# Row sums stored with a step, a guard on one engine, and a new order list in a two-layer attention kernel

## The chip, the cores and the metric

The kernel runs on one core of a Trainium2 chip, as one program in one launch. Its time is the device time in microseconds (us) of that core. What is compared is the median over runs of each kernel. One execution was also taken with the hardware profiler; its rows are what is read below.

The core has TensorE (matrix products into PSUM), VectorE, ScalarE and GpSimd (elementwise work; GpSimd doesn't reach PSUM) and SyncE, whose queue SP issues nearly all the DMAs here. In the rows they are PE (its weight loads PEld), DVE, ACT, POOL and SP.

## What is computed

The first layer is an attention with sinks and a window, 4 batches of 8 heads, 768 positions of 64 values; the second is a mixture of 4 attention experts over its result, of which each row takes the best two.

```python
keep = is_sink | in_window                 # 4 sinks, window 128
scores = np.where(keep, scale * q @ k.T, -1e9)
a = np.exp(scores - scores.max(-1))
a = a / (a.sum(-1) + 1e-9)
x = a @ v                                  # first layer, all heads side by side: 768 x 512
...
logits = x @ w_gate                        # 4 experts, the best 2 kept, softmax over them
for e in range(4):                         # causal attention of each expert
    q, k, v = x @ wq[e], x @ wk[e], x @ wv[e]
    a = exp(masked(scale * q @ k.T) - max)
    a /= a.sum(-1) + 1e-9
    out += weight[e] * (a @ v @ wo[e])
```

All is in float32. The `1e-9` under each row sum is the *guard* of this document.

## The kernel before, in words

**Work units.** The first layer goes by pairs of heads (16 of them: 4 batches of 4), each in blocks of 128 rows. Rows 0 and 1 of a pair form one unit (`first_rows`, L1051), rows 2 and 3, and 4 and 5, one each (`both_rows`, L1112). The second layer goes by pairs of experts (8 of them): `first_rows` for rows 0 and 1, `wide_rows` (L940) for rows 2 to 5. In each unit TensorE makes scores in PSUM (L713, L721, L730); VectorE masks them and takes the row minimum of the negated scores (`low`, L987, L1069, L1131); ScalarE takes the exponential and the row's sum (`exp`, L999, L1074, L1135); then comes the factor; GpSimd or ScalarE multiplies by it (L1007, L1009, L1086, L1089, L1155); and the result is transposed, either by TensorE (L791) with evacuations, or by VectorE and a trip through DRAM (out L834 and L926, back L838 to L923), for the product with v (L757, L762). Batch 0 of the first layer comes first, with its q and k transposed by TensorE (`turn_by_pe`, L683); after that a batch's second layer lies beside the next batch's first. The second layer's projections are three-pass products (L1244 for q and k, L1271 for v, L1320 for the output).

**The row statistics.** Each unit holds one tile `st` of 128 partitions by 20 values (six exist), seen as 5 rows of 4: row 0 the minimum, row 1 the sum, row 2 the factor, row 3 a partial minimum. A row has 2 or 4 values in use, side by side. Row 4 is filled with 1e-9 at the start (L465) and nothing reads it. The factor is made by `factor` (L770) in two steps, and in the second layer by a third: the guard adds 1e-9 to the 2 or 4 sums, on VectorE or GpSimd as the list says; VectorE takes the reciprocal; GpSimd multiplies by the row's expert weight:

```python
on = nc.gpsimd if guarded.eng == POOL else nc.vector
on.tensor_scalar(st.t[:, 2, :w], st.t[:, 1, :w], 1e-9, None, op0=OP.add)
...
nc.vector.reciprocal(st.t[:, 2, :w], st.t[:, 2, :w])
```

**The order.** Each piece of work is a step of a planner (`plan.step`), with a cost in ns for each engine that may do it; there are 2514. The text `ORDER` names them all in the order in which they are issued. A letter behind a number chooses the engine (`a` ScalarE, `v` VectorE, `p` GpSimd) or, with `q`, another tile shape on TensorE; without one the step goes to the first engine of its costs. Every engine takes its own steps in that order and waits at each for what it needs. So the list alone sets what is queued behind what. The costs, the waits for a DMA to land (`lag`, `BACK_LATE`, `LOAD_LATE`) and the clock that `emit` (L259) keeps from them serve to make a list; with a list given they still set which buffer a step gets and where spare products (L373, L375) go while TensorE would be idle.

**TensorE's tile shapes.** A step has a mode: `quad` works on 64x64 tiles, four side by side; `rows` and `ROWS` on two halves of the rows; `cols` on two halves of the columns; `FULL` on the whole array. The product with the sinks (L762) may be `FULL` or `rows`.

## Time and profile before

| | |
|---|---|
| runs shown | 346.21, 346.69, 346.72 us |
| median | 346.69 us |
| profiled execution | 345.65 us |
| its span, first to last instruction | 343.9 us |
| granted TensorE clock, mean over the span | 1.000 |
| busy in the span: TensorE, VectorE, ScalarE, GpSimd | 98%, 83%, 76%, 63% |
| guards on VectorE, on GpSimd | 39, 49 |

Busy shares are means over stages with different limits. TensorE counts as busy while a product is under way, and the ends of products are modelled, so a second look by stretch is needed. A row of the grouped view gives line, engine, operation, destination<-source by tile name, shapes and count, then the busy time in us and the mean duration in ns of one, and behind the second bar the engine's idle time just before them and who ended it. In the view of one line the three numbers are the shortest, the middle and the longest duration in ns. A row of the timeline gives the start and the length in us, and in brackets the idle time before it.

### The profile page before, as it was taken

To read this page: it belongs to the slowest core of one execution; us is meant where nothing else is said; L and a number is where in the kernel's file an instruction comes from. 1 tells how busy PE (TensorE), PEld (TensorE's weight loads), DVE (VectorE), ACT (ScalarE), POOL (GpSimd) and SP (SyncE) were. 2 spreads that over 40 slices of the span, in tenths; PEclk is the share of its full clock that TensorE was granted. 3 is DMA by queue.
4 is the path that set the end of the run, shared out by engine and by line. 5 is a ranking of instruction groups with operands and counts; after the bars stand their busy time and mean duration, and the time that the engine had idled before them with its cause. 6 is when DMAs were issued, how large, how long until landed. Compare 5 with 4: busy or idle time off the path is not lost.

```text
span 343.9 us, 12484 instructions
## 1 busy us (share of the span) xinstructions
PE 336.1 (98%) x4292; PEld 292.9 (85%) x4292; DVE 285.6 (83%) x1198; ACT 263.1 (76%) x871; POOL 216.9 (63%) x481
## 2 busy tenths in 40 slices
PE   8989999999999999999999999999999999999996
PEld 7777888987997889988889889987898899987885
DVE  4999999889998997899896997898888964489721
ACT  3999999879968978479868874599958868259822
POOL 6789998987956747758683744287687700285500
PEclk9999999999999999999999999999999999999999
DMA  6999589797968779878966778759775283057667
GB/s 179 248 202 163 99 166 171 177 205 182 300 181 203 248 178 156 234 152 173 279 194 131 218 225 181 231 110 254 231 211 181 80 266 126 2 191 202 208 201 274
DMA packets 159319, 65.45 MB, mean 190 GB/s; under 512 B 115856, under 2 KB 148880, under 8 KB 159256
## 3 DMA queue, kind: packets, MB, share of 16 engines
q1 hardware_dynamic: 158984, 64.53, 74.1%
q8 instruction: 34, 0.56, 0.7%
q14 instruction: 29, 0.24, 0.2%
q10 hardware_dynamic: 272, 0.13, 0.1%
HBM read 39.69 MB, written 24.90 MB: 188 GB/s over the span
## 4 chain that ended last, share of the span: by engine, by line
PE 82%; POOL 6%; DMA 4%; DVE 2%; ACT 2%; issue 1%; SPq 1%; ACTq 0%; POOLq 0%; DVEq 0%
PE b L757 20%; PE b L1244 20%; PE b L1320 10%; PE b L1271 8%; PE b L721 7%; PE b L791 6%; PE b L730 5%; PE b L713 2%; PE b L762 2%; DMA n<-in_v_dram 1%; DMA n<-in_q_dram 1%; POOL n L1089 1%; DMA p<-d 1%; POOL p L1155 1%; SPq L1198 1%
## 5 line engine op out<-in xcount | busy, mean ns | idle before, releaser
L1135 ACT ACTIVATE p<-p,st 128x132 f32<-128x132 f32 x128 | 51.0, 404 | 0.4 <-DVE st L1131 0.2
L1074 ACT ACTIVATE n<-n,st 128x128 f32<-128x128 f32 (+1 forms) x96 | 42.9, 449 | 4.1 <-DVE st L1069 3.9
L721 PE MATMUL b<-ks,qs 64*128 64x384 f32 (+3 forms) x384 | 39.6, 336 | 0.0
L1089 POOL TENSOR_TENSOR n<-n,st 128x256 f32<-128x256 f32 (+2 forms) x48 | 33.8, 714 | 4.9 <-DVE st L779 3.8
L1271 PE MATMUL b<-wvh,x 128*128 128x260 f32 x192 | 36.4, 284 | 0.0
L999 ACT ACTIVATE n<-n,st 128x768 f32<-128x768 f32 (+1 forms) x32 | 28.1, 878 | 10.5 <-DVE st L987 10.2
L776 POOL TENSOR_SCALAR st<-st 128x4 f32<-128x4 f32 (+1 forms) x49 | 11.0, 224 | 37.3 <-ACT n L999 19.2
L757 PE MATMUL b<-n,v 128*64 128x128 f32 x544 | 34.1, 274 | 0.2 <-issue 0.2
L1320 PE MATMUL b<-woh,y 128*128 128x512 f32 (+1 forms) x100 | 34.2, 396 | 0.0
L1155 POOL TENSOR_TENSOR p<-p,st 128x512 f32<-128x512 f32 x32 | 33.3, 1046 | 0.2
L721 PEld LDWEIGHTS b<-ks,qs 64*128 64x128 f32 x384 | 31.1, 186 | 2.5 <-issue 0.7
L1244 PE MATMUL b<-x,wqh 128*128 128x256 f32 (+1 forms) x128 | 32.9, 342 | 0.3 <-DVE st L987 0.3
L1244 PE MATMUL b<-x,wkh 128*128 128x512 f32 (+1 forms) x128 | 33.2, 343 | 0.0
L1131 DVE CUSTOM_DVE_ANT_0 p<-b,pair_mask 128x132 f32<-128x132 f32 x128 | 32.2, 284 | 0.2
L757 PEld LDWEIGHTS b<-n,v 128*64 128x64 f32 x544 | 30.2, 137 | 2.1 <-issue 1.4
L609 ACT ACTIVATE n<-b 128x384 f32<-128x384 f32 (+2 forms) x65 | 26.7, 439 | 7.0 <-PE b L683 4.6
L1271 PEld LDWEIGHTS b<-wvh,x 128*128 128x128 f32 x192 | 30.2, 188 | 0.7 <-DVE st L1069 0.4
L932 POOL TENSOR_SCALAR_AFFINE_SELECT p<-p 128x256 f32<-128x256 f32 x48 | 21.0, 461 | 14.0 <-DMA p<-d 13.6
L831 DVE STREAM_TRANSPOSE n<-n 128x768 f32<-128x768 f32 (+1 forms) x32 | 28.2, 897 | 1.1 <-ACT n L1007 0.5
L609 ACT ACTIVATE p<-b 128x256 f32<-128x256 f32 (+2 forms) x53 | 22.4, 447 | 8.0 <-PE b L1320 7.3
L730 PE MATMUL b<-n,n 64*64 64x196 f32 (+1 forms) x512 | 27.4, 337 | 0.0
L702 DVE STREAM_TRANSPOSE n<-n 128x384 f32<-128x384 f32 x48 | 26.7, 563 | 0.8 <-DMA n<-in_k_dram 0.8
(147 smaller groups left out, 1028.4 us busy)
## 6 DMA issues: line engine op xcount, KB each, us to landing
d<-n SPq DMA_DIRECT2D x24, 288.0 KB
n<-in_v_dram SPq DMA_DIRECT2D x16, 384.0 KB
p<-d SPq DMA_DIRECT2D x96, 64.0 KB
d<-n SPq DMA_DIRECT2D x16, 384.0 KB
n<-d SPq DMA_DIRECT2D x64, 96.0 KB
out_dram<-p SPq DMA_DIRECT2D x23, 256.0 KB
d<-n SPq DMA_DIRECT2D x16, 320.0 KB
n<-d SPq DMA_DIRECT2D x64, 80.0 KB
```

Source lines behind the costliest of these rows:

```text
L609: nc.scalar.activation(dst(), src(), AF.Copy)
L721: nc.tensor.matmul(o, self.qs.t[hs, a, qs], x, start=n == 0, stop=n == 2)
L730: nc.tensor.matmul(o[c:c + 64, 256 * r:256 * r + n], self.q_of()[hs, q:q + 64], self.ks.t[hs, 0, k:k + n], start=True, stop=True)
L757: nc.tensor.matmul(o[e * 64:e * 64 + 64], lhs, rhs, start=e not in self.begun, stop=last and self.done == len(self.steps))
L1074: nc.scalar.activation(x, x, AF.Exp, bias=st.t[:, 0, n:n + 1], scale=-1.0, accum_out=st.t[:, 1, n:n + 1])
L1089: nc.gpsimd.tensor_mul(x, x, f[:, :, None].to_broadcast([128, n, 128 * i + 128]))
L1131: nc.vector.tensor_tensor_reduce(out=p.t[:, n, :], in0=s2[e].t[:, 324 * r:324 * r + SW], in1=pair_mask, scale=-scale, scalar=BIG, op0=OP.a ...
L1135: nc.scalar.activation(p.t[:, n, :], p.t[:, n, :], AF.Exp, bias=st.t[:, 0, n:n + 1], scale=-1.0, accum_out=st.t[:, 1, n:n + 1])
L1155: nc.gpsimd.tensor_mul(p.t[:, :, :128], p.t[:, :, :128], f()[:, :, None].to_broadcast([128, 4, 128]))
L1244: nc.tensor.matmul(t.t, w[a][:, c, es], X[b, c].t[:, x, cs], start=c == 0 and m == 0, stop=c == NCH - 1 and m == 2)
L1271: nc.tensor.matmul(t.t[:, :VW], X[b, c].t[:, a, qs], W["wv"][w][:, c, :], start=c == 0 and n == 0, stop=c == NCH - 1 and n == 2)
L1320: nc.tensor.matmul(t.t[:, a0:z0], Y[b, c].t[:, a, qs], W["wo"][w][:, c, a0:z0], start=c == 0 and n == 0, stop=c == EP - 1 and n == 2)
```

## The change

- The tile `st` is seen through a new function `stats`: value n of row r lies at 5n + r, so the 2 or 4 values of a row are 20 bytes apart. All three makers of `st` use it. The six fills of row 4 go.
- The guard is always on VectorE. The planner's costs of guard and reciprocal, of `clean` and of the band's second mask get new numbers.
- `first_rows` of the first layer may, by `q` in the list, make its scores in 64x64 tiles (`quarters`): two column halves, one after the other, in place of one.
- The planner takes loads of q, k and v to land 100 to 500 ns later than before, and read-backs from DRAM 300 ns later.
- The list is a new one, from the first words on. By counting its words: guards on VectorE 39 to 88, on GpSimd 49 to 0; evacuations on ScalarE 147 to 145 (of 210); normalisations on ScalarE 45 to 50 (of 128); diagonal masks on VectorE 7 to 10 (of 16); remainders of weights on VectorE 2 to 4 (of 16); sink products in `rows` mode 16 to 24 (of 32); first-row scores in `quad` mode 0 to 6 (of 16 that may).

```diff
--- before.py
+++ after.py
@@ -37,102 +37,102 @@
 PSUM = ("b",)
 ORDER = """
-47 3 45 46 53 50 55a 48 51v 136 134 57 135 60 52a 54v 62a 58a 56 59v 61v 65 66 139 68 70 67 72 82 223 1 141a 83 88 69 142 108
-71 73 144a 4 0 143v 84 86 87 146 89 74p 147a 114 137 109 75 110 117 148v 228 140a 149 115 5 230a 145 314 150a 320 229v 91 77
...
+3 45 47 46 48 53 50 57 52a 136 51v 55v 225 134 54a 56 58v 60 65q 135 314 0 59v 61v 231 142 62v 66 72 143v 70 68 232v 233a 67
+73 144a 82 139 141a 1 83 88 137 84 86 69 91 89 234 71 74 140v 320 146 108 148a 145 75 321v 77 149 85 87 147v 109 92 114 110
...
@@ -394,6 +394,10 @@
             return x.rearrange(f"p ({names}) -> p {names}", **dict(zip("abcde", dims))) if len(dims) > 1 else x
         return Buf(tag, view)
+    def stats():
+
+        return Buf("st", lambda slot: slots["st"][slot].rearrange("p (n r) -> p r n", r=5))
+
     def psum_cost(n, copies=1):
         return {DVE: 70 + 1.04 * n + 60 * (copies - 1), ACT: 52 + 0.833 * n + 60 * (copies - 1)}
@@ -461,8 +465,6 @@
             row_mask[i] = m
     cmask = consts.tile([128, 512], F32, name="cmask")
     lmask = consts.tile([128, 384], F32, name="lmask")
-    for t in slots["st"]:
-        nc.vector.memset(t[:, 16:20], 1e-9)
     tril = consts.tile([128, E, E], F32, name="tril")
     below = consts.tile([128, E], F32, name="below")
@@ -489,7 +491,7 @@
         for sign, base in ((1, 0), (-1, 15)):
             nc.gpsimd.affine_select(out=sel, in_=sel, pattern=[[-16 * sign, 2]], compare_op=OP.is_ge, fill=0.0, base=base,
                                     channel_multiplier=sign)
-    CLEAN = [plan.step(5.0, {POOL: 2250}, clean)] if banded else []
+    CLEAN = [plan.step(5.0, {POOL: 2860}, clean)] if banded else []
     LMASK = [plan.step(6.0, {POOL: 1600}, lots_of_mask)]
     RANKS = [plan.step(7.0, {POOL: 490}, ranks)]
@@ -703,12 +705,16 @@
                                new, [nat] + [x for x in used if x is not nat], fifo="kx" if new else None)]
             self.ready[which].append((lo, hi, steps, self.sinks(which, lo, prio, steps)))
-        def scores(self, outs, i, ks, lots=False):
+        def scores(self, outs, i, ks, lots=False, quarters=False):
             qs = slice(i * 128, i * 128 + 128)
             if self.exact:
                 k = self.part(1, ks.start // 128, ks.stop // 128)
-                for e, o in enumerate(outs):
+                for h in range(2 if quarters else 0):
+                    for e, o in enumerate(outs):
+                        hs, c = slice(e * 64, e * 64 + 64), slice(h * 64, h * 64 + 64)
+                        nc.tensor.matmul(o[c].rearrange("p (j c) -> p j c", c=128), self.q_of()[hs, i * 128:i * 128 + 128][:, c], k[hs], start=True, stop=True)
+                for e, o in enumerate(() if quarters else outs):
                     hs = slice(e * 64, e * 64 + 64)
                     nc.tensor.matmul(o.rearrange("p (j c) -> p j c", c=128), self.q_of()[hs, qs], k[hs], start=True, stop=True)
                 return
@@ -772,13 +778,12 @@
             return st.t[:, 2, :w] if w == 2 else st.t[:, 2, :w].rearrange("p (i e) -> p i e", e=2)
         def guard():
-            on = nc.gpsimd if guarded.eng == POOL else nc.vector
-            on.tensor_scalar(st.t[:, 2, :w], st.t[:, 1, :w], 1e-9, None, op0=OP.add)
+            nc.vector.tensor_scalar(st.t[:, 2, :w], st.t[:, 1, :w], 1e-9, None, op0=OP.add)
         def go():
             nc.vector.reciprocal(st.t[:, 2, :w], st.t[:, 2, :w])
-        guarded = plan.step(prio, {DVE: 140, POOL: 150}, guard, after, (), [st])
-        s = plan.step(prio, {DVE: 145}, go, [guarded], (), [st])
+        guarded = plan.step(prio, {DVE: 76}, guard, after, (), [st])
+        s = plan.step(prio, {DVE: 88}, go, [guarded], (), [st])
         if weight:
             s = plan.step(prio, {POOL: 150}, lambda: nc.gpsimd.tensor_mul(of_heads(), of_heads(), weight()),
                           [s] + weight_after, (), [st])
@@ -931,7 +936,7 @@
                 half = slice(2 * g, 2 * g + 2)
                 nc.gpsimd.affine_select(out=pts[1].t[:, half], in_=pts[0].t[:, half], pattern=[[32, 2], [64, 2], [0, 2], [1, 32]],
                                         compare_op=OP.is_ge, fill=0.0, base=0, channel_multiplier=-1)
-        cut_off = plan.step(prio, {POOL: 800}, tri, [came], [pts[1]], [pts[0]])
+        cut_off = plan.step(prio, {POOL: 848}, tri, [came], [pts[1]], [pts[0]])
         band_products(prio, acc, i, lambda c, g, e: pts[c].t.rearrange("p (g h) (r e) c -> p g e r h c", g=2, r=2)[:, g, e],
                       [lambda g=g: sk.t[:, 128 * g:128 * g + 128].rearrange("p (h r c) -> p r h c", h=2, r=2) for g in range(2)], pts, sk, [came], [came, cut_off],
                       value, diff, vs, made_vs)
@@ -952,7 +957,7 @@
                 continue
             cols, mask = blocks[i], masks[i]
             n = len(cols)
-            st = buf("st", 5, 4)
+            st = stats()
             if n <= 2:
                 ps, sums = [buf("p", 2, n * 128)] * 2, []
             else:
@@ -1052,15 +1057,15 @@
         def flat(x):
             return x.rearrange("p a c -> p (a c)")
-        st, p, pt, s2, t = buf("st", 5, 4), buf("n", 6, 128), buf("n", 6, 128), two(512), two(8, 64)
+        st, p, pt, s2, t = stats(), buf("n", 6, 128), buf("n", 6, 128), two(512), two(8, 64)
         lows, sums, norms, moved = [], [], {}, []
         def go():
             for i in range(2):
-                pair.scores([x.t[:, 128 * i:256 * i + 128] for x in s2], i, slice(0, 128 * i + 128))
+                pair.scores([x.t[:, 128 * i:256 * i + 128] for x in s2], i, slice(0, 128 * i + 128), quarters=mm.mode == "quad")
         inputs = list(dict.fromkeys(pair.inputs(0, [0]) + pair.inputs(1, [0, 1])))
         mm = plan.step(prio - leads[0], {PE: score_cost(128, pair.exact) + score_cost(256, pair.exact) + 37}, go, inputs, s2,
-                       [pair.qs, pair.ks], fifo="s", mode="rows")
+                       [pair.qs, pair.ks], fifo="s", mode="rows", alt=("quad", 700) if pair.exact and banded else None)
         for i in range(2):
             for e in range(2):
                 n, w = 2 * i + e, 128 * i + 128
@@ -1113,7 +1118,7 @@
-        st, p, sums, lows, s2 = buf("st", 5, 4), buf("p", 4, SW), [], [], two(512)
+        st, p, sums, lows, s2 = stats(), buf("p", 4, SW), [], [], two(512)
         inputs = list(dict.fromkeys(pair.inputs(i, range(i - 1, i + 2)) + pair.inputs(i + 1, range(i - 1, i + 2))))
         mm = plan.step(prio - LEAD_S, {PE: 58 + 8 * NW / 2.4}, lambda: pair.near([x.t for x in s2], i), inputs, s2,
                        [pair.qs, pair.ks], fifo="s", mode="quad")
@@ -1210,7 +1215,7 @@
                 before = [x[2][0] for x in loaded[-1]]
                 loaded[-1].append((a, z, [plan.step(
                     load_prio + (0.1 if n else 0.2 if which == 2 else 0), {ACT: 1900} if early else {SP: 550 if which == 2 else 500 if by_pe else 2300}, load, (), [] if n else [t],
-                    [t] if n else [], moves=((320 if by_pe else 305) if which == 2 else LONG_NS[z - a] if by_pe else 435) * (z - a), behind=before, fifo=None if n else tag, lag=1500 if early else 300 if by_pe else 0 if which == 2 else LOAD_LATE)]))
+                    [t] if n else [], moves=((320 if by_pe else 305) if which == 2 else LONG_NS[z - a] if by_pe else 435) * (z - a), behind=before, fifo=None if n else tag, lag=1500 if early else 400 if by_pe else 500 if which == 2 else LOAD_LATE)]))
                 if whole and which == 1 and not n:
                     FIRST.append(loaded[-1][0][2][0])
         pair.qs = nat[0]
@@ -1352,7 +1357,7 @@
     SWAPPED, AWAY_NS, BACK_NS = (5, 6), 178, 240
     SELECT_NS = 375
     AWAY = [(b, hp, i) for b in range(1, B) for hp in range(HP) for i in (2, 4)]
-    BACK_LATE, LOAD_LATE = 450, -500
+    BACK_LATE, LOAD_LATE = 750, -100
     SPLIT = {5: [(0, 3), (3, 5)], 6: [(0, 3), (3, 6)]}
     ORD = "1 0 p0 2 3 p1"
```

## Rows read from the trace of the kernel before

**Rows 1.** The page's busy us, share of the span, instructions of each engine
```profile
PE 336.1 (98%) x4292; PEld 292.9 (85%) x4292; DVE 285.6 (83%) x1198; ACT 263.1 (76%) x871; POOL 216.9 (63%) x481
```

**Rows 2.** The page's chain that ended last: share of the span by engine
```profile
PE 82%; POOL 6%; DMA 4%; DVE 2%; ACT 2%; issue 1%; SPq 1%; ACTq 0%; POOLq 0%; DVEq 0%
```

**Rows 3.** Table by stretch: length, busy us (count) of PE, PEld, DVE, ACT, POOL; clock; DMA
```profile
10.00:50.00 40.00, 37.73 (x788) 30.35 (x779) 39.32 (x198) 38.30 (x164) 35.41 (x73) 1.00 0.93 174
50.00:130.00 80.00, 78.76 (x964) 68.90 (x964) 74.01 (x327) 68.38 (x233) 60.10 (x139) 1.00 0.83 204
130.00:320.00 190.00, 190.00 (x2090) 167.72 (x2088) 157.89 (x629) 142.45 (x444) 111.00 (x235) 1.00 0.69 184
320.00:344.00 24.00, 20.75 (x274) 18.12 (x270) 8.69 (x17) 9.59 (x23) 3.74 (x5) 1.00 0.66 221
```

**Rows 4.** Waits of TensorE: who waited for whom, us in total, times, longest
```profile
PE b L791 <- DVE st L1069: 0.9, 1, 0.9
PE b L757 <- DMA n<-in_v_dram: 0.8, 1, 0.8
```

**Rows 5.** The view of line 776, guards: shortest, middle, longest ns
```profile
L776 POOL TENSOR_SCALAR st<-st x49: 216/223/234, 10.3 to 318.9; 128x4 f32<-128x4 f32 x30, 128x2 f32<-128x2 f32 x19
L776 DVE TENSOR_SCALAR st<-st x39: 125/167/1523, 19.9 to 315.9; 128x4 f32<-128x4 f32 x26, 128x2 f32<-128x2 f32 x13
```

**Rows 6.** The view of line 779, reciprocals
```profile
L779 DVE RECIPROCAL st<-st x88: 122/166/179, 10.6 to 320.9; 128x4 f32<-128x4 f32 x56, 128x2 f32<-128x2 f32 x32
```

**Rows 7.** Timeline of all engines around 20 us
```profile
19.90 1.52 DVE L776 TENSOR_SCALAR st<-st 128x4 f32<-128x4 f32 x1
...
20.14 1.26 POOL L1035 TENSOR_TENSOR p<-n 128x512 f32<-128x512 f32 x1
...
22.09 0.33 PE L791 MATMUL b<-ident,psk 64*128 64x64 f32 x3 [0.95 <-DVE st L1069]
```

**Rows 8.** Timeline of VectorE around 125.6 us
```profile
125.57 0.24 DVE L776 TENSOR_SCALAR st<-st 128x4 f32<-128x4 f32 x2
125.71 0.29 DVE L1131 CUSTOM_DVE_ANT_0 p<-b,pair_mask 128x132 f32<-128x132 f32 x1
```

**Rows 9.** Groups by line, 0 to 50 us: guards
```profile
L776 DVE TENSOR_SCALAR st<-st 128x4 f32<-128x4 f32 x8 | 3.8, 481 | 0.1
L776 POOL TENSOR_SCALAR st<-st 128x4 f32<-128x4 f32 x5 | 1.1, 226 | 2.1 <-ACT p L1135 1.4 <-ACT n L1074 0.5
```

**Rows 10.** Groups by line, 50 to 130 us: guards on GpSimd
```profile
L776 POOL TENSOR_SCALAR st<-st 128x4 f32<-128x4 f32 (+1 forms) x18 | 4.1, 225 | 4.5 <-ACT n L999 2.3 <-ACT n L1074 0.8 <-ACT p L999 0.4
```

**Rows 11.** Groups by line, 130 to 344 us: guards
```profile
L776 DVE TENSOR_SCALAR st<-st 128x4 f32<-128x4 f32 (+1 forms) x25 | 7.3, 298 | 4.4 <-ACT p L1135 1.8 <-ACT n L999 1.7 <-ACT n L1074 0.9
L776 POOL TENSOR_SCALAR st<-st 128x4 f32<-128x4 f32 (+1 forms) x26 | 5.8, 223 | 30.7 <-ACT n L999 16.8 <-ACT p L999 8.9 <-ACT p L1135 2.5
```

**Rows 12.** Groups by line of VectorE, whole span
```profile
L1305 DVE RECIPROCAL gate<-gate 128x6 f32<-128x6 f32 x4 | 0.8, 194 | 0.1
...
L465 DVE MEMSET st<- 128x4 f32 x6 | 0.1, 62 | 0.0
```

**Rows 13.** Groups by line of GpSimd, whole span
```profile
L1155 POOL TENSOR_TENSOR p<-p,st 128x512 f32<-128x512 f32 x32 | 33.3, 1046 | 0.2
...
L1035 POOL TENSOR_TENSOR p<-n 128x512 f32<-128x512 f32 x16 | 20.6, 1287 | 1.7 <-DMA n<-in_v_dram 1.4
```

**Rows 14.** Timeline of TensorE, 26 to 28 us
```profile
26.04 0.93 PE L713 MATMUL b<-n,n 64*128 64x128 f32 x8
26.90 0.90 PE L730 MATMUL b<-n,n 64*64 64x196 f32 x16
27.73 0.46 PE L791 MATMUL b<-ident,n 64*128 64x64 f32 x8
```

**Rows 15.** The chain in order of time: start us, us, what
```profile
49.72 8.64 PE b L1244 x48
...
102.76 5.08 DMA n<-in_v_dram
...
226.53 2.89 PE b L730 x64
```

More of the change, by code (lines that the diff above doesn't have):

```diff
@@ new lines @@
+1309 904 913 914 905 707 1013 1019 889 791 757 915 828q 827 964 890 829 1028 966p 758 830 831 1051 1187 1034 970 965a 780
+1199 1188 917 1200 916 708 1029 1057 918 919 1030 1037 920 849 1052 967 1035 1189 1053 922p 950 1055 891p 906 36 781 971 851
+1201 1020 1079 850 1038 921a 1009 1190 1202 852 894a 1056 907a 923 1191 1058 1077 948 968 44v 1021 893p 1060 1203 892a 1192
+1036 1032 908p 909 1204 895 924v 910a 853 911v 1022 896a 925a 1061 1084 897v 1211 854 1085 927 1089 1101 928v 1212 1214 951
+1054 1059 1218 972 929a 1124 898 1087 912 926 930 1023 969 1003 1033 1031 1107 1125 1130 1062 1310 38 1063 1213 1126 1086
@@ new lines @@
+1229a 1355q 1481 1536 1486 1534 1300 1404 1535 1403 1537 1538 1450 1426 1405 1357 1499 1554 1358 1406a 1407a 1451q 1539 1611
+1540 1500 1517 1501 1452 1608 1230 1284 1376 1541 1910 1542 1612 1543 1262 1487 1485 1544a 1483 1546 1427 1545a 1258 1518
+1408 1488 1555 1503 1377 1502 1244 1549 1556 1489 1490 1429 1263 1285 1428q 1430 1609 1616 1519 1301 1614 1520 1557 1453
+1378q 1379 1504 1505 1559 1618 1550 1561 1547 1651 1521a 1558 1454 1380 1431 1652 1264 1628 1381 1657 1726 1560 1653 1836
+1562 1714 1655 1563 1727 1654 1619 1720 1564 1565a 1728 1615 1613 1617 1715 1721 1304 1567 1493a 1492a 1732 1506 1629 1658
@@ L136 @@
+2298 2418v 2419v 2433a 2317 2420 2318 2434 2439 2440 2359 2460 2461 2489 2485 2497 2480 2486 2493 2498 2499a 2361 2482 2481
+2494 2483 2196 2188 2490 2362 2487v 2484 2491a 2495a 2505 2180 2200 2500 2501 2184 2488 2506 2502 2507a 2492 2496 2508 2509
+2503a 2510 2512v 2511v 2504 2513
 """
```

169 lines of the change are left out of this document (75 added, 94 removed), and 6 rows, old and new, of the table ORDER.

## The prediction, made before the changed kernel ran

> **What bounds the kernel now.** I read the page's busy line first, then the table by stretch, then what ended TensorE's waits, then the guard's own rows. TensorE is busy 336.1 of 343.9 us [rows 1], but a busy TensorE isn't one at its peak, so the chain of waits comes next: 82% of it lies on TensorE, the rest on GpSimd, DMA, VectorE and ScalarE [rows 2]. The table by stretch says where that rest lies [rows 3]. From 10 to 50 us everything is full at once: VectorE 39.32 of 40, ScalarE 38.30, TensorE 37.73, GpSimd 35.41. Here the first batch's attention has little matmul work to lay beside its softmax, and VectorE, with 0.68 us idle, sets the pace. From 50 to 130 TensorE lacks 1.24 us. From 130 to 320 it lacks nothing (190.00 of 190) while VectorE has 32 us spare. The 3.25 us at the end are the last store after the last product. So a gain has to come before 130 us, or from fewer or shorter products. The longest single TensorE waits after the start agree: VectorE 0.9, a load of v 0.8 [rows 4].
>
> **The guard (1e-9) and the row sums.** Before, 39 guards run on VectorE and 49 on GpSimd; after, all 88 on VectorE with a step of 20 bytes.
> A guard on VectorE takes 125 ns at least, 167 in the middle, 1523 at most, although all do the same; the reciprocal on the same tile never passes 179 [rows 5, 6]. The 1.52 us one shows why [rows 7]: issued at 19.90, it ends at 21.42 when it has outlasted GpSimd's L1035 (20.14 to 21.40), and TensorE waits 0.95 us for what is queued behind it. A free guard occupies VectorE for 70 ns (two of them, 125.57 to the next start at 125.71 [rows 8]).
> In 0 to 50 us, 8 guards on VectorE take 3.8 us and 5 on GpSimd take 1.1 [rows 9]. Held to the 167 ns of a free one, the eight would take 1.3, so 2.5 us are waiting. VectorE's time for them is 2.5 + 8 x 0.07 = 3.1 us; after, 13 x 0.07 = 0.9, if a strided guard doesn't wait. That frees 2.2 us of the engine that sets the pace. What is late next is ScalarE, with 40 - 38.30 = 1.7 us idle: beyond that it binds. I take **-1.7 us** (ends: 0, if ScalarE already binds at every step; -2.2).
> From 50 to 130 us 18 guards go from GpSimd to VectorE and 6 were there [rows 10]; VectorE has 6 us idle there and TensorE's waits aren't theirs: 0. After 130 us, 25 guards with 7.3 us [rows 11] lie beside 32 us of idle VectorE and a full TensorE: 0.
> Does the step cost anything in itself? No row of before has a 20-byte step. Reciprocal: the nearest row is L1305, 6 elements 16 bytes apart, 194 ns [rows 12], against 166 for L779, so 0 to 28 ns, over the first 13 some 0.4 us; the 0.5 us between 2.2 and 1.7 covers it. GpSimd's multiplications read the factor strided; between a factor read over and over (L1155, 1046 ns) and a second full stream (L1035, 1287) lie 0 to 241 ns each [rows 13]; eight fall in the first batch, at most 1.9 us, and GpSimd has 4.6 idle. I take 0 for both. A gain can't be excluded either; the range's low end holds it. The six memsets that go cost 62 ns each [rows 12], at the start, while VectorE waits for the first data: 0.
>
> A page rule speaks against the main term. The Trainium skill, "Vector Engine (DVE) Microarchitecture Reference", section 5.1, gives a one-source operation both SBUF ports when source and destination lie in SBUF and the outermost count is even; it names no step, and says that steps above 2 weren't measured. Its page "SBUF — State Buffer", section "SBUF: two separate sides", has the pair shared with GpSimd locked for a whole instruction. The trace agrees on the lock for the packed guard (1.52 us) and can't tell for a strided one; by the rule a strided guard of 2 or 4 elements waits as before, and the sum is that of the second rival.
>
> **The list.** Sorting its 595 TensorE steps by tile shape (64x64, two row halves, two column halves, whole array), consecutive steps change shape 147 times instead of 154; 23 instead of 30 in the first 50 steps, 124 both times behind them. Six first-row score steps (five among the first 52) are now cut into 64x64 tiles like their neighbours. A near-score step takes 0.83 us from its start to the next one's when the shape changes (26.90 to 27.73) and 2.89/4 = 0.72 in a run [rows 14, 15], so a change costs about 0.11: 7 x 0.11 = 0.8 us. A first-row step before a near-score step takes 0.86 (26.04 to 26.90), by the run's price 0.72: 5 x 0.14 = 0.7. Both fall where TensorE has 2.3 us idle and waits for the others: 0, and -1.5 if TensorE binds there.
> Loads and read-backs are only *planned* to land 100 to 500 ns later, which moves their consumers down the list: the middle distance from a read-back to its first product grows from 10 to 11.5 TensorE steps (the wide tiles, 32 of them) and from 7.5 to 8 (the bands, 24). On SP's queue the first batch's first load of v goes behind nearly all q and k loads of the other pairs, whose transposes come earlier on TensorE. What a later landing can save is the wait at 107 us, where v lands 5.08 us after its issue at 102.76 [rows 15]: 0.8 us. I take **-0.8** (ends: 0, another transfer is late instead; -1.2, all that TensorE lacks from 50 to 130).
> The split of other work barely moves: five more normalisations on ScalarE, two fewer evacuations, three more masks and two more weight rests on VectorE; behind 50 us both engines have room, and before it I can't place them. The other edited numbers are the planner's; they issue nothing.
>
> **Sum.** -1.7 - 0.8 = -2.5 us on the profiled execution's 345.65 (span 343.9 plus 1.75 around it) gives 343.15. The runs' median, 346.69, lies 1.04 above the profiled one, so I forecast 344.2; with the ends, 346.69 - 4.9 = 341.8 (2.2 + 1.2 + 1.5) to 345.9 (the load alone).
>
> **Rivals.**
> *The wait for ScalarE moves to VectorE (slower).* GpSimd stood idle before its guards until the exponentials were done: 2.1 us before 50, 4.5 to 130, 30.7 after [rows 9 to 11]. On VectorE such a wait holds up what is queued behind it: score reductions, evacuations, transposes, for whose banks TensorE waits. Against it: the 39 guards on VectorE had 4.5 us of idle time, nearly all after 130 us, and the new list leaves a middle of 3 VectorE steps between the last exponential and the guard (2.5 before). If half of the 6.6 us before 130 stays, TensorE is 3.3 later: 346.69 + 3.3 - 2.5 = 347.5. It decides from 2.5 us of such waits.
> *A strided guard still waits for GpSimd (the change doesn't do what it says).* Then 13 early guards wait 2.5/8 = 0.31 us each, 4.1 instead of 2.5: +1.6; less 0.8 for the load: 347.5. For it: nothing in the trace shows a strided one beside a long GpSimd operation; against: nothing but the reciprocal, which doesn't wait though it is packed.
> *The room is taken at once.* ScalarE binds from 10 to 50 us, another transfer is late in v's place: 346.5. For it: 1.7 us of idle ScalarE only.
> *The start goes better than its parts.* TensorE's 2.3 us of idle time between 10 and 50 us and the 1.5 of shapes come back whole, and 1.2 behind: 346.69 - 5.0 = 341.7, and below where GpSimd's 1.1 counts too, 340.6.
>
> **How the numbers follow.** A measurement of this kernel can tell about 0.2%, 0.7 us, from no change: same is 346.0 to 347.4. Forecast 0.52 (faster 0.51, same 0.01). The better start 0.08, all faster. Room taken 0.15 (same 0.10, faster 0.05). Wait on VectorE 0.14 (slower 0.12, same 0.02). Guard still waits 0.11 (slower 0.10, same 0.01). Together faster 0.64, same 0.14, slower 0.22. The likeliest case alone spans 341.8 to 345.9; for 8 in 10 I go to 341.2 below, into the better start, and to 347.8 above, past both slower cases' middle.
>
> **What would show it.** L776 on VectorE 88 times with no duration above 0.25 us, also beside a GpSimd operation of 1 us, shows the main step right; durations up to 1.5 us show the second rival. The stretch 10 to 50 us should have its products some 1.7 us earlier (the first three-pass projections, L1244, start near 48 us instead of 49.72 [rows 15]), with ScalarE nearly without idle time. TensorE's wait for v should be gone. From 130 us on the two kernels should run at one distance; if that shrinks, a wait has come in where none was. Idle time in front of L776 on VectorE, above 2.5 us before 130, shows the first rival. The forecast is wrong if 10 to 50 us isn't shorter, whatever the end says.

## The result: slower by 4.8 us, and the profile after

On one chip the changed kernel took 351.51 us in the median (350.62 to 352.82), the kernel before 346.71: a ratio of 1.0142 [1.0108, 1.0177]. The forecast was 344.2 in a range that ended at 347.8. The ratio and its 95% interval are estimated from the single runs of both kernels, so it can differ by some 0.2% from the ratio of the two medians. The profiled execution is one of 350.62 us, with a span of 348.9 and TensorE's clock at 1.00 throughout, so 5.0 us are to be found against the one shown of before.

The page of the kernel after: busy us, share and instructions of each engine, then the chain that ended last by engine. TensorE has 50 more products (4342) than in [rows 1], GpSimd 17 us less work. In the chain VectorE has risen from 2% to 16% [rows 2].
```profile
PE 338.3 (97%) x4342; PEld 293.2 (84%) x4342; DVE 292.9 (84%) x1248; ACT 264.9 (76%) x874; POOL 200.0 (57%) x422
...
PE 68%; DVE 16%; DMA 6%; issue 3%; ACT 2%; POOL 2%; SPq 2%; DVEq 0%; POOLq 0%; ACTq 0%
```

The table by stretch, columns as in [rows 3]. From 10 to 50 us every engine did less than before: TensorE 36.19 against 37.73, VectorE 37.00 against 39.32. From 130 to 320 TensorE was full before; now it lacks 1.24 us, with VectorE still 30 us idle.
```profile
10.00:50.00 40.00, 36.19 (x758) 28.64 (x760) 37.00 (x197) 36.02 (x153) 31.98 (x63) 1.00 0.90 164
50.00:130.00 80.00, 79.80 (x962) 68.98 (x958) 76.97 (x347) 69.17 (x237) 55.85 (x120) 1.00 0.92 203
130.00:320.00 190.00, 188.76 (x2115) 166.94 (x2110) 159.54 (x648) 141.69 (x439) 97.94 (x196) 1.00 0.68 175
320.00:349.00 29.00, 25.54 (x300) 21.50 (x298) 13.15 (x33) 14.19 (x36) 7.29 (x13) 1.00 0.76 254
```

The guard is now L781 and the reciprocal L784 (shortest, middle, longest ns, as in [rows 5, 6]). All 88 guards are on VectorE with their step of 20 bytes, and the longest still takes 1376 ns; the reciprocal on the same tile never passes 182.
```profile
L781 DVE TENSOR_SCALAR st<-st x88: 125/167/1376, 10.6 to 323.8; 128x4 f32<-128x4 f32 x56, 128x2 f32<-128x2 f32 x32
...
L784 DVE RECIPROCAL st<-st x88: 121/168/182, 10.9 to 324.7; 128x4 f32<-128x4 f32 x56, 128x2 f32<-128x2 f32 x32
```

The trace's records of the guards beside those of GpSimd show what they wait for. All 22 that take more than 250 ns end 24 to 30 ns after a GpSimd operation does. Mostly it is the one that runs when the guard is issued; the longest, at 143.83 us, stands through that one and the two that follow it. None of the other 66 is issued with more than 300 ns of a GpSimd operation still to run. Of the 88 reciprocals on the same tile 14 are, and none of those waits.

The groups by line of VectorE from 0 to 50, 50 to 130 and 130 to 349 us: guards, with busy us, mean ns and the idle time before them, as in [rows 9 to 11].
```profile
L781 DVE TENSOR_SCALAR st<-st 128x4 f32<-128x4 f32 x12 | 3.6, 306 | 0.5 <-ACT p L1140 0.4
...
L781 DVE TENSOR_SCALAR st<-st 128x4 f32<-128x4 f32 (+1 forms) x25 | 5.5, 224 | 0.9 <-ACT n L1004 0.9
...
L781 DVE TENSOR_SCALAR st<-st 128x4 f32<-128x4 f32 (+1 forms) x51 | 14.0, 287 | 6.0 <-ACT p L1004 3.3 <-ACT n L1004 1.8 <-ACT p L1140 0.6
```

TensorE's waits (who waited for whom; us in total, times, longest). The 0.8 us for a load of v [rows 4] are gone. New are two waits for "issue", that is for nothing the profile shows, and one of 0.6 for VectorE's score reduction. The 0.8 for a load of q stands at 5.5 us, before the first score step; in the traces of e16 and e17 below, which have the same list, it is missing, so it is not counted as an effect of the change.
```profile
PE b L736 <- issue: 1.6, 1, 1.6
PE b L685 <- issue: 1.2, 1, 1.2
...
PE b L685 <- DMA n<-in_q_dram: 0.8, 1, 0.8
PE b L719 <- DVE st L1136: 0.6, 1, 0.6
PE b L763 <- DVE st L992: 0.5, 1, 0.5
```

The timeline of all engines at that third wait, cut to its rows (start, length, what). The guard is issued at 235.50, while GpSimd is in the first of two multiplications (L1014, two in 2.89 us), and takes 1.25, until that multiplication ends. The next score reductions (L1136) stand behind it in VectorE's order; they start at 236.66, and TensorE, whose next scores need a bank that they empty, stands 0.56 us.
```profile
235.26 2.89 POOL L1014 TENSOR_TENSOR n<-n,st 128x768 f32<-128x768 f32 x2
...
235.50 1.25 DVE L781 TENSOR_SCALAR st<-st 128x4 f32<-128x4 f32 x1
...
236.66 0.28 DVE L1136 CUSTOM_DVE_ANT_0 p<-b,pair_mask 128x132 f32<-128x132 f32 x1
...
237.23 0.92 PE L719 MATMUL b<-n,n 64*128 64x128 f32 x6 [0.56 <-DVE st L1136]
```

The timeline of TensorE at the other two. It stands from 10.0 us, after most of a run of transposes, and from 15.3 us in the middle of a score step, of whose 16 products 10 have begun.
```profile
8.74 1.24 PE L685 MATMUL b<-ident,n 64*64 64x64 f32 x46
11.16 0.46 PE L685 MATMUL b<-ident,n 64*64 64x64 f32 x16 [1.18 <-issue]
...
14.59 0.73 PE L736 MATMUL b<-n,n 64*64 64x196 f32 x9
16.93 0.39 PE L736 MATMUL b<-n,n 64*64 64x200 f32 x3 [1.62 <-issue]
```
Counted from TensorE's first record (weight loads, products and semaphores), the gaps stand in front of instructions 449 and 705, which are 256 apart. The trace has packets of 16,384 bytes on a queue of kind "instruction" (q8) at these times: they land at 9.86 and 15.69 us, and TensorE goes on 1.30 and 1.24 later. Before, they landed at 8.69 and 13.80, and instructions 449 and 705 ran at 10.50 and 16.21 without such a gap. The traces of all 20 kernels of this document bear it out: at the numbers that follow in steps of 256 TensorE never goes on sooner than 1.06 us after the packet of the same rank has landed (663 places), and at 449, 705 and 961 it stands over 0.4 us 26 times, each time until 1.06 to 1.60 us after the landing. So TensorE had run out of instructions and waited for these packets; that the queue's packets are TensorE's instructions is inferred from these numbers and times. The Trainium skill, "Runtime: NRT & Kernel Launch", section "Instruction fetch mechanics", has instructions fetched in blocks of 256 and calls the crossing mostly hidden; the 256 agree, the hiding doesn't hold in the changed kernel's first 17 us.

How far a kernel is behind, in us: the time at which TensorE has begun the same share of its work, less that of the kernel before. Idle products are left out, and each product is priced by the mean duration of its shape in the kernel before. The 64x64 first-row products, which the kernel before lacks, are priced at half of the row halves that they replace; that price is a choice, and another one moves the rows with them by over 1 us up to 98 us. Rows with the same products can be compared with each other without it, and e3 (guards and the new list, without these products) needs no such price. Worked out from the trace records of one execution each; differences under 1 us carry nothing. The runs named here follow below.
```
                      at  17    55    98   151   244 us of before
after                    1.5   2.2   2.5   3.4   4.5
e3 no 64x64 steps        1.5   2.1   2.5   5.6   5.7
e17 no early guards      0.9   0.2   1.1   2.8   3.4
e18 no late guards       1.6   2.3   1.4   1.9   1.3
e16 no guards            0.9   0.2   1.2   1.3   2.8
e9 start of old list     0.7   4.8   4.4   9.5  10.1
e7 old list, no guards   0.0  -0.9  -0.5   0.5   0.1
```

### The profile page after: what moved, and what is told of

The parts are those of the page before. It is cut to its first block, busy times and chain, and to the rows that moved or that the text cites. A ratio compares the mean times of both kernels' runs of the same rounds, so it can differ in the third digit from the quotient of the medians.

```text
span 348.9 us, 12599 instructions
## 1 busy us (share of the span) xinstructions
PE 338.3 (97%) x4342; PEld 293.2 (84%) x4342; DVE 292.9 (84%) x1248; ACT 264.9 (76%) x874; POOL 200.0 (57%) x422
## 4 chain that ended last, share of the span: by engine, by line
PE 68%; DVE 16%; DMA 6%; issue 3%; ACT 2%; POOL 2%; SPq 2%; DVEq 0%; POOLq 0%; ACTq 0%
PE b L763 20%; PE b L1249 13%; PE b L1276 8%; PE b L727 7%; PE b L1325 6%; PE b L796 5%; DMA n<-in_k_dram 4%; PE b L736 4%; DVE p L1136 3%; PE b L719 2%; DVE n L992 2%; PE b L768 2%; SPq L1203 2%; DVE st L781 2%; DMA d<-n 1%
## 5 line engine op out<-in xcount | busy, mean ns | idle before, releaser
L727 PE MATMUL b<-ks,qs 64*128 64x384 f32 (+3 forms) x384 | 42.1, 338 | 0.1
L1094 POOL TENSOR_TENSOR n<-n,st 128x256 f32<-128x256 f32 (+2 forms) x46 | 32.9, 727 | 5.7 <-DVE st L784 4.9
L727 PEld LDWEIGHTS b<-ks,qs 64*128 64x128 f32 x384 | 32.4, 186 | 3.4 <-issue 1.5
L763 PE MATMUL b<-n,v 128*64 128x128 f32 x544 | 34.9, 275 | 0.0
L1249 PE MATMUL b<-x,wkh 128*128 128x512 f32 (+1 forms) x128 | 33.3, 344 | 0.0
L1249 PE MATMUL b<-x,wqh 128*128 128x512 f32 (+1 forms) x128 | 33.2, 343 | 0.0
L1136 DVE CUSTOM_DVE_ANT_0 p<-b,pair_mask 128x132 f32<-128x132 f32 x128 | 32.3, 283 | 0.2
L1152 POOL TENSOR_TENSOR psk<-p,st 128x32 fp32r<-128x32 f32 x32 | 8.1, 252 | 41.3 <-DVE st L784 32.2
L611 ACT ACTIVATE p<-b 128x256 f32<-128x256 f32 (+1 forms) x53 | 22.7, 456 | 10.9 <-PE b L1325 9.9
L781 DVE TENSOR_SCALAR st<-st 128x4 f32<-128x4 f32 (+1 forms) x88 | 23.1, 272 | 7.3 <-ACT p L1004 3.3
```

The lines of the kernel that those rows point to most:

```text
L611: nc.scalar.activation(dst(), src(), AF.Copy)
L727: nc.tensor.matmul(o, self.qs.t[hs, a, qs], x, start=n == 0, stop=n == 2)
L763: nc.tensor.matmul(o[e * 64:e * 64 + 64], lhs, rhs, start=e not in self.begun, stop=last and self.done == len(self.steps))
L1094: nc.gpsimd.tensor_mul(x, x, f[:, :, None].to_broadcast([128, n, 128 * i + 128]))
L1136: nc.vector.tensor_tensor_reduce(out=p.t[:, n, :], in0=s2[e].t[:, 324 * r:324 * r + SW], in1=pair_mask, scale=-scale, scalar=BIG, op0=OP.a ...
L1249: nc.tensor.matmul(t.t, w[a][:, c, es], X[b, c].t[:, x, cs], start=c == 0 and m == 0, stop=c == NCH - 1 and m == 2)
```

## The experiments

Times are medians; ratios are to the kernel before, run beside each of them, whose median was 346.4 to 347.3 us. Savings in per cent are differences of two ratios.

### Does the strided guard wait for GpSimd, and what do the waits cost?

**e1_no_lock.** The guard becomes a second reciprocal, of the same shape and place.
```diff
-            nc.vector.tensor_scalar(st.t[:, 2, :w], st.t[:, 1, :w], 1e-9, None, op0=OP.add)
+            nc.vector.reciprocal(st.t[:, 4, :w], st.t[:, 1, :w])
...
-            nc.vector.reciprocal(st.t[:, 2, :w], st.t[:, 2, :w])
+            nc.vector.reciprocal(st.t[:, 2, :w], st.t[:, 1, :w])
```


> The changed kernel, in which the guard's instruction is a second reciprocal of the same 2 or 4 values (row 1 to the unused row 4) and the factor is the reciprocal of the bare sum; the addition of 1e-9 is left out. The number and place of VectorE's instructions stay. Theory A (two causes: 2.6 us of the 4.9 are lost before 20 us, where TensorE runs out of instructions; the other 2.3 come later, where a strided guard waits for GpSimd's operation as a packed one does): no L781 above 0.2 us, the steps of 1.0 us near 146 and 1.1 us near 236 us go, and the time falls by 2.3 us (1.5 to 3.5) to 349.2. Theory B (the list alone is slower: loads of k and a full VectorE from 45 to 63 us; the guards' waits lie beside other work): 351.5, within 0.7.


Measured: 349.13 us, 1.0066 [1.0033, 1.0099]. Its line in place of the guard (the view of one line) has no long one:
```profile
L781 DVE RECIPROCAL st<-st x88: 125/169/185, 11.0 to 320.5; 128x4 f32<-128x4 f32 x56, 128x2 f32<-128x2 f32 x32
```
So an operation that doesn't wait for GpSimd, put in the guard's place, saves 0.76% (2.6 us, give or take 1.7); half of the loss stays. The edit also frees the factor from waiting for the guard's result; what that is worth by itself isn't shown. But 20 of these reciprocals are issued with over 300 ns of a GpSimd operation still to run and none waits, so it is the operation and not its place that makes a guard wait.

**e2_packed.** The changed kernel with `st` packed as before.
```diff
-        return Buf("st", lambda slot: slots["st"][slot].rearrange("p (n r) -> p r n", r=5))
+        return Buf("st", lambda slot: slots["st"][slot].rearrange("p (r n) -> p r n", r=5))
```


> The changed kernel with the four values of a row of st side by side again; nothing else is changed. Theory A (the step does nothing to the wait): 351.5 within 0.7, and L781 again near 23 us in 88, up to 1.4 us. Theory C (the step takes away part of the waits, and without it they are more): L781 above 26 us in all, and slower by over 1 us.


Measured: 351.81 us, 1.0145 [1.011, 1.018], the same as strided; the guard's row (same view) is the same too within some ns. No effect of the step shows, on the wait or on the time.
```profile
L781 DVE TENSOR_SCALAR st<-st x88: 120/168/1357, 10.9 to 324.0; 128x4 f32<-128x4 f32 x56, 128x2 f32<-128x2 f32 x32
```

**e7_no_guard_before, e8_no_guard_no_quad, e16_no_guard_quads.** The 88 guards left out: of the kernel before (there both lines of the guard go), and of the changed one without and with its 64x64 first-row steps.
```diff
-            nc.vector.tensor_scalar(st.t[:, 2, :w], st.t[:, 1, :w], 1e-9, None, op0=OP.add)
+            pass
...
-            nc.vector.reciprocal(st.t[:, 2, :w], st.t[:, 2, :w])
+            nc.vector.reciprocal(st.t[:, 2, :w], st.t[:, 1, :w])
```


> The kernel before without the 88 guards: the reciprocal reads the sums. Each sum holds the exponential of 0, so it is at least 1, and in float32 adding 1e-9 to it changes nothing. Theory A: 39 operations that stand for 6.5 us in all and 49 of GpSimd with their two hops go, TensorE's wait at 20.9 us (1.2) with them: 345.2 (344.0 to 346.2). Theory B (all of it covered): 346.6 within 0.7.

> The changed kernel without the 88 guards (sums of at least 1, so nothing changes in float32) and with its six first-row score steps in two row halves. Theory A: the guards' 2.3 us and some 0.4 of the stalls go, and what is left above the kernel before is the rest of the stalls: 348.6 (347.5 to 349.8), the stalls at TensorE's instructions 449 and 705 there again. Theory B (the list alone): 351.5.

> The kernel after without its 88 guards (1e-9 left out; the sums are at least 1), with its six 64x64 first-row steps, which the earlier run without guards had not. If the 64x64 steps cost through TensorE's instruction supply: 0.5 or more above that run's 348.0 (ratio 1.0024 to the kernel before). If they are worth nothing either way: 1.0024 within 0.002.


Measured: e7 345.31 us, 0.9956 [0.9929, 0.9983], faster than both kernels; e8 347.98, 1.0024 [1.0, 1.0049]; e16 348.35, 1.0025 [0.9993, 1.0057]. No effect of the 64x64 steps shows. The three make an account in per cent of before: guards cost 0.44 in the old list and 1.17 in the new one, where all are on VectorE; the lists without guards differ by 0.69. So +1.17 - 0.44 + 0.69 = +1.42: of 4.9 us some 2.5 are the guards' move (give or take 1.9) and 2.4 the list (give or take 1.5). The list's part holds whatever else was changed with it: order, engines of other work, buffers.

**e17_no_early_guards, e18_no_late_guards.** Which guards? The changed kernel without its first 12 guards (before 50 us), and without the other 76.
```diff
+            if plan.steps.index(guarded) not in LEFT:
-            nc.vector.tensor_scalar(st.t[:, 2, :w], st.t[:, 1, :w], 1e-9, None, op0=OP.add)
+                nc.vector.tensor_scalar(st.t[:, 2, :w], st.t[:, 1, :w], 1e-9, None, op0=OP.add)
...
-            nc.vector.reciprocal(st.t[:, 2, :w], st.t[:, 2, :w])
+            nc.vector.reciprocal(st.t[:, 2, :w], st.t[:, 1 if plan.steps.index(guarded) in LEFT else 2, :w])
```


> The kernel after without its first 12 guards, those before 50 us (1e-9 left out in them; the sums are at least 1); the other 76 stay on VectorE. If the early guards, on an engine without idle time, carry the guards' loss: nearly all of the 3.3 us that leaving out all 88 gave back, so 348.2 to 349.2 (ratio near 1.005). If the late ones carry it: 351.0 to 351.7.

> The kernel after without its last 76 guards (1e-9 left out in them; the sums are at least 1); the first 12 stay on VectorE. If the early guards carry the guards' loss: 351 or a little less. If the late ones do: 348.2 to 349.2. If the two parts add up: this run and the run without the first 12 save 3.3 us together.


Measured: e17 350.62 us, 1.0093 [1.006, 1.0125]; e18 348.16, 1.0039 [1.0011, 1.0067]. Leaving out the early ones saves 0.49% (1.7 us, give or take 1.7), the late ones 1.03% (3.6, give or take 1.5). Together that is 1.52%, against 1.17% for all 88; the difference of 0.35 (give or take 0.64) doesn't tell whether the parts add. That the early ones carry it, as I expected of an engine without idle time, is a miss: the late ones weigh more. The stretch from 130 to 320 us, in the table by stretch of e17 and then of e18, shows the late part: TensorE lacks 1.15 us in the one and nothing in the other.
```profile
130.00:320.00 190.00, 188.85 (x2098) 166.56 (x2094) 158.90 (x649) 141.88 (x438) 98.01 (x197) 1.00 0.67 176
```
```profile
130.00:320.00 190.00, 190.00 (x2119) 168.27 (x2115) 151.37 (x607) 143.67 (x444) 99.36 (x200) 1.00 0.69 179
```
In the shares of e18's chain, from its page, VectorE is down from 16% to 2%.
```profile
PE 90%; DMA 3%; DVE 2%; SPq 2%; ACT 1%; issue 1%; DVEq 0%
```
TensorE's idle time there is no measure of the guards alone: it is 1.2 us of the 3.6, and e16, which has no guards, lacks 1.6 us in the same stretch, in one wait for a tile read back from DRAM (TensorE's waits in e16, 130 to 320 us). Where the rest of the 3.6 us lies isn't shown.
```profile
PE b L763 <- DMA n<-d: 1.6, 1, 1.6
```

### Is it the move, or the place in the list?

**e4_all_vector, e6_all_vector_no_lock.** The kernel before, with nothing changed but its 49 GpSimd guards put on VectorE at their old places; e6 with a second reciprocal for the guard, as in e1.
```diff
-            on = nc.gpsimd if guarded.eng == POOL else nc.vector
-            on.tensor_scalar(st.t[:, 2, :w], st.t[:, 1, :w], 1e-9, None, op0=OP.add)
+            nc.vector.tensor_scalar(st.t[:, 2, :w], st.t[:, 1, :w], 1e-9, None, op0=OP.add)
```


> The kernel before, its list and its packed tile, with the 49 guards of GpSimd given to VectorE and nothing else. Theory A (each guard behind which GpSimd is busy holds VectorE until that operation ends): L776 88 times, some 25 us in all, TensorE's wait at 20.9 us stays, and 1 us more is lost (0 to 2.5): 347.7. Theory B (guards' waits are covered): 346.7 within 0.7. The moved guards also wait on VectorE for the exponentials; if that is dear, the time is above 349.

> The kernel before with all 88 guards on VectorE (355.8 us with its guards as they are), each replaced by a second reciprocal that leaves out the 1e-9. Theory A (the waits for GpSimd cost what the move cost): 347.0 (345.5 to 348.5). Theory D (what costs is that VectorE stands at the guard until ScalarE's exponentials are done, with its queue behind it): 353 to 356.


Measured: e4 355.78 us, 1.026 [1.0226, 1.0293], far above what I expected; e6 350.46, 1.0099 [1.0064, 1.0135], between the two theories. So in the old list the waits for GpSimd cost 1.6% (give or take 0.5). The other 1.4% against e7 (give or take 0.4) are 88 operations in VectorE's order that wait for no GpSimd operation: they take their own time, and VectorE stands at them until an exponential is done. How it divides between the two isn't shown. The view of e4's guards (what their engine's idle time before them waited for) has 10.2 us of it in four rows, against 4.5 for the 39 of before [rows 9, 11]; 9.9 us of it lie behind 130 us.
```profile
L775 DVE TENSOR_SCALAR st<-st x88: 127/169/1297, 10.9 to 328.2; 128x4 f32<-128x4 f32 x56, 128x2 f32<-128x2 f32 x32
...
  ACT p L1134: 3.7, 8
  ACT n L998: 2.9, 4
  ACT p L998: 2.0, 3
  ACT n L1073: 1.6, 3
```

**e13_list_alone, e14_five_early_back, e15_late_back.** The reverse: the changed kernel with guards back on GpSimd at their places in the new list: the 49 of before; the five of them that are among the first 12; the other 44.
```diff
-            nc.vector.tensor_scalar(st.t[:, 2, :w], st.t[:, 1, :w], 1e-9, None, op0=OP.add)
+            on = nc.gpsimd if guarded.eng == POOL else nc.vector
+            on.tensor_scalar(st.t[:, 2, :w], st.t[:, 1, :w], 1e-9, None, op0=OP.add)
```


> The kernel after with the same 49 guards on GpSimd as before, each at its place in the new list; 39 stay on VectorE. So the new list, strides, 64x64 steps and all, without the move of the guards. If the move is the cause (the guards' waits on VectorE): 348.2 (347.2 to 349.2). If the list, above all its gaps in TensorE's instructions at the start, costs by itself: 350.5 to 352. If the new list needs its guards on VectorE, because GpSimd's queue stands at a guard: above 352.

> The kernel after with five guards alone back on GpSimd, those of the first 12 in the list that GpSimd had before (all before 50 us). If the loss comes from VectorE in the first 50 us, where it sets the pace: most of the 3 us that are lost by 50 us come back, 349.5 or less. If the early loss is TensorE's instruction gaps: 351 to 352, since those stand before the first of these guards can matter.

> The kernel after with the other 44 of the 49 guards back on GpSimd, all after the first 12; the first 12 stay on VectorE. If the late long waits (143.83, 169.55, 235.50 us in the kernel after) cost by themselves: 350 (the loss after 130 us, 1.9 us, goes). If they are covered by TensorE's queue: 351.5.


Measured: e13 359.23 us, 1.0341 [1.0305, 1.0377]; e14 352.0, 1.0125 [1.009, 1.0161]; e15 357.66, 1.0315 [1.0269, 1.0361]. The time of e13 is that of its third case: in the new list GpSimd's queue stands at a guard. The view of e13's guards agrees: GpSimd's guards themselves are short, but VectorE's reciprocals wait 7.2 us for them, and GpSimd stands idle before them, waiting for exponentials, for 51 us in the four rows, with its work behind them held up. In the kernel before, GpSimd stood 37 us before its 49 guards too [rows 9 to 11], so the idle time alone doesn't prove the cost. Moving the five early ones makes no difference that shows. So the 49 guards together can't change engine at their places in either list without loss, and these three don't measure the move by itself; e7 and e16 to e18, which leave guards out, come nearer.
```profile
L782 POOL TENSOR_SCALAR st<-st x49: 217/228/276, 10.7 to 332.9; 128x4 f32<-128x4 f32 x30, 128x2 f32<-128x2 f32 x19
...
  ACT n L1005: 23.6, 11
  ACT p L1005: 13.3, 6
  ACT p L1141: 9.4, 9
  ACT n L1080: 4.8, 5
...
  DVE st L785: 7.2, 9
```

### What are the gaps at 10 and 15 us worth?

**e3_no_quad, e5_more_warm.** e3 is the changed kernel with its six 64x64 first-row steps in row halves again (the `q` behind six words goes). e5 has four times as many idle products before the first data, a quarter as wide.
```diff
-        for n in range(WARM):
-            nc.tensor.matmul(idle.t[:, n % 4, :], nought, nought, start=True, stop=True)
+        for n in range(4 * WARM):
+            nc.tensor.matmul(idle.t[:, n % 4, :32], nought, nought[:, :32], start=True, stop=True)
```


> The changed kernel with its six first-row score steps in two row halves, as before: 8 products and 8 weight loads instead of 16 and 16 each, the order unchanged. Theory A (TensorE's instructions come in blocks of 256, each some 5 us after the block before it has been begun, and the early steps use one up in 3.6 to 3.8 us): two of the steps lie before the second stall, so 16 and 32 instructions fewer, at 14 to 20 ns each: both stalls (1.4 and 1.9 us) stay at TensorE's instructions 449 and 705 and shrink by 0.2 to 0.6 in all; 351.0 (350.2 to 351.6). Theory B (the stalls wait for loaded data): they stay at the same products, 351.5.

> The changed kernel, in which the idle products at the very start are cut into quarters: 24 of 32 columns instead of 6 of 128, so 72 more instructions of TensorE in the same time; their result is used by nothing. Theory A (instructions are supplied in blocks): the two stalls stay at TensorE's instructions 449 and 705, that is 72 instructions earlier in the program's work, and the time grows by 72 x 20 ns = 1.4 us to 352.9 (351.8 to 353.6). Theory B (data): they stay at the same products, instructions 521 and 777, and the time is 351.5 within 0.7.


Measured: e3 351.21 us, 1.0139 [1.0089, 1.019]; e5 358.5, 1.0347 [1.0304, 1.039], a miss on the time, since a narrow idle product takes as long as a wide one (last section) and the work began 7.5 us later. For the gap both tell the same: with other instructions ahead of it, it stays in front of the same number, not of the same work. In e3 instructions 449 and 705 come 1.49 and 1.17 us after the ones before them. In e5 449 comes after 13 transposes of a step, 35 products sooner in the work. The second gap is gone there: its packet landed at 19.50 us, 1.49 us before TensorE came to 705.
```profile
15.97 0.58 PE L685 MATMUL b<-ident,n 64*64 64x64 f32 x13
17.27 0.95 PE L685 MATMUL b<-ident,n 64*64 64x64 f32 x44 [0.71 <-issue]
```

**e9_old_start, e10_old_start_long, e11_old_start_no_guard, e12_old_start_long_no_guard.** The changed kernel with the first 160 or 300 words of its list as in the old one, order and engine letters both, guards excepted (24 of the 160 and 40 of the 300 words so take another engine or tile shape), and the remaining words in the new order; with guards and without.
```diff
 ORDER = """
-3 45 47 46 48 53 50 57 52a 136 51v 55v 225 134 54a 56 58v ...
+47 3 45 46 53 50 55a 48 51v 136 134 57 135 60 52a 54v 62a ...
```


> The kernel after, with the first 160 words of its list (some 25 of 595 TensorE steps, up to about 17 us) put back in the order of the list before; the other 2354 words stand in the order of the new list, guards all on VectorE and strided. Theory (the new list's start asks for TensorE's instructions faster than they arrive): the two issue gaps of TensorE before 17 us go, TensorE's instructions 449 and 705 start near 10.5 and 16.2 us as in the kernel before, and the time falls from 351.5 to 349.0 (348.2 to 350.0). Rival (the gaps belong to the program as a whole or are made good or lost again later): gaps at the same two numbers, or none, and 350.8 to 352.

> As the run before, but the first 300 words (some 45 TensorE steps, up to about 26 us) in the order of the list before. If the start alone counts: 349.0, within 0.5 of the run before. If what follows the gaps in the new list's first 300 words costs or saves too: 1 us or more away from it.

> The kernel after with the first 160 words in the old order and without the 88 guards (1e-9 left out; the sums are at least 1). If the guards' waits and the start are the two causes and add up: 351.5 less 2.5 less 2.5, so 346.3 (345.4 to 347.2), no slower than the kernel before. If a third cause as large as either is left: 348 or more.

> The kernel after with the first 300 words in the old order and without the 88 guards (1e-9 left out). By the two causes 346.3 again, within 0.5 of the run with 160 words; against the old list without guards (345.3) it tells what the rest of the new list is worth: -1 to +1.


Measured: e9 355.27 us, 1.0228 [1.019, 1.0266]; e10 354.04, 1.0201 [1.0159, 1.0242]; e11 349.87, 1.0079 [1.0051, 1.0107]; e12 347.31, 0.9997 [0.997, 1.0024]. The gaps went as expected (in e9 instruction 449 starts at 10.58 without one, 705 at 17.23 after 0.16 us), and the time rose: the expectation for e9 and e10 fails, and my theory of two causes that add up with it. The guards of 0 to 50 us in e9, by line, take 8.1 us of VectorE instead of the 3.6 of the kernel after:
```profile
L786 DVE TENSOR_SCALAR st<-st 128x4 f32<-128x4 f32 x12 | 8.1, 681 | 0.2 <-ACT p L1145 0.2
```
With all guards on VectorE the old start makes them meet GpSimd's long operations; the new start has less of that and runs into the gaps. What the gaps are worth in the end isn't shown. e16, which has them and no guards, is 0.9 us behind at 17 us and 0.2 at 55 (the table of distances), and its ratio can't be told from e12's; e11, without gaps and guards, is 0.54% slower than e16 (give or take 0.43). So closing the gaps by going back to the old start gained nothing that shows.

An order with fewer TensorE instructions in the first 17 us and the guards at places free of GpSimd's long operations wasn't tried.

## Why the prediction was wrong

- **"13 x 0.07 = 0.9, if a strided guard doesn't wait"** is the step on which the -1.7 us stood, and it failed: the strided guard waits as the packed one does (1376 ns; e2 the same at 1357). Counted as the sum counted (what exceeds 167 ns, plus 0.07 us each), the 12 guards of the first 50 us took 1.7 + 0.8 = 2.5 us of VectorE, not 0.9. For the guards the mechanism of the second rival, given 0.11, is the true one. The Trainium skill, "Vector Engine (DVE) Microarchitecture Reference", section 5.1, names no step among its conditions for the use of both ports; it lists steps above 2 as not measured, and the runs here show the wait with a step of 5. I let the lack of a strided row in the trace weigh more than the absence of a reason why a step should matter.
- **"After 130 us, 25 guards with 7.3 us lie beside 32 us of idle VectorE and a full TensorE: 0"**, and the same for 50 to 130: failed, and dearer. The 76 guards behind 50 us take 19.5 us, and without them the kernel is 3.6 us faster (e18, give or take 1.5). An engine's share of idle time didn't cover a guard of 1.25 us that stood in its order ahead of what TensorE needed next, as at 235.50; that one cost TensorE 0.56 us. This is why the second rival's 347.5 was too low as well: it priced the early 13 alone, and like the forecast it had nothing for the list.
- **"The list ... 0"**: failed. The lists without guards differ by 0.69% (e7 and e16), 2.4 us (give or take 1.5). I counted changes of tile shape and not TensorE instructions: by its 100th word the new list has 13 transpose steps of q and k where the old one has 10, and TensorE outran its instructions twice. How the 2.4 us divide between these gaps, later orders, engines and buffers stays open: closing the gaps in e12 gives 0.28%, within its uncertainty, and in e11 the time rises.
- **-0.8 for the load of v**: the wait is gone, as forecast, and from 50 to 130 us TensorE lacks 0.20 us instead of 1.24. In the time it doesn't show. In the terms of the sum, then, the guards came out at some +2.5 instead of -1.7 and the list at +2.4 instead of 0.
- **Shapes, 64x64 steps, strided reciprocals and factors at 0**: no run speaks against it. e3, e8 and e16 show nothing for the steps, e2 nothing for the stride; the reciprocal's middle is 168 ns against 166.
- **The first rival (VectorE stands at the guards for ScalarE)**: in the new list no. The idle time before L781 is 1.4 us before 130, less than the 2.5 named as its threshold. With all guards on VectorE in the old list such waits come to some 10 us (e4), but 1.1 of them before 130; the rest lies behind 130 us, where the rival had put no price. What they cost there isn't shown by itself.
- **What would show it**: three signs spoke against the forecast: guards above 0.25 us; the first three-pass product (L1249) at 51.78 us instead of 49.65; a distance that grows behind 130 us (2.5 us at 98, 3.4 at 151, 4.5 at 244). VectorE's 39.32 busy us of 40 [rows 3] looked like a limit that the change would lift; after, it is busy for 37.00 and less is done.

## What to carry to other kernels

Before moving a small operation to another engine, list which operations of a third engine it will wait for at its new time, and price the longest single wait by what stands behind it in order, however idle the engine is on average. Moving an operation and writing a new order are one change: each list here loses 2 to 3% when 49 of its guards change engine at their old places (e4, and e13 against the changed kernel). Leaving the operation out, where its effect is below the last digit of float32, is the only variant that beat both kernels (e7, 0.9956).

## What the runs showed of the hardware that I had not expected

- An addition of 2 or 4 elements on VectorE, from SBUF to SBUF, waits for a running GpSimd operation, packed (up to 1357 ns, e2) or with a step of 20 bytes (up to 1376). The longest stands through three GpSimd operations that follow each other; the one at 235.50 gets in ahead of the second of two. What decides this isn't shown. A reciprocal of the same tile at the same place doesn't wait (185 ns at most in e1).
- TensorE can run out of instructions early in a kernel. It stands in front of fixed numbers, 256 apart, until 1.06 to 1.60 us after a packet of 16,384 bytes has landed (26 waits of over 0.4 us in the 20 traces). In the changed kernel it had gone through the 256 up to 705 in 3.8 us (11.16 to 14.99), ahead of the packet; before, it took 5.7 us, and the packet had landed 2.4 us earlier. In e5 it took 3.7 us (17.27 to 20.98) and stood for nothing: the packet had landed at 19.50.
- An idle product with 128x128 weights costs nearly the same with 32 columns as with 128: 48 with 32 columns took 10.45 us (0.22 each) in e5, 12 with 128 columns 2.93 (0.24 each) in the changed kernel. The row is from e5's timeline of TensorE.
```profile
1.12 10.45 PE L1342 MATMUL b<-nought 128*128 128x32 f32 x48 [1.12 <-DVE nought L409]
```
